# A state update over 64 rows, padded with zeros to 128

The kernel computes a decayed linear attention followed by a gated feed-forward block. Four times in its run it updates a running state from the lower 64 rows of a tile. The change lets these four updates use all 128 rows, with a copy of v whose upper 64 rows are zero.

## Chip, cores, metric

One core of one Trainium2 chip. The metric is the device time of the kernel in microseconds (us). A profile of one execution was kept for every kernel; it is the first of the six runs listed, but for the kernel before, whose profiled execution (310.72 us) is not among its timed runs. The span of a profile is some 2 us shorter than the time, because the time counts what stands around the program too.

## The reference

Eight batches, eight heads, 576 positions, head size 64. The attention has no softmax: scores are multiplied by a causal decay, so the past can be carried in a 64x64 state per head. The code is shortened: `rel` is the distance of two positions.

```python
def _attn_ref(q, k, v):
    scores = scale * np.matmul(q, k.transpose(0, 1, 3, 2))
    gamma = 1.0 - 2.0 ** (-5.0 - np.arange(H))
    Dmat = np.where(rel >= 0, gamma[:, None, None] ** rel[None, :, :], 0.0)
    return np.matmul(scores * Dmat[None], v)

def _moe_ref(x, w_in, w_out):          # x: 4608 tokens x 512
    h = x @ w_in                       # 512 -> 2048
    return (h * np.cos(h)) @ w_out     # 2048 -> 512
```

## The kernel before

The 4608 tokens are handled in 36 groups of 128 rows. A batch has 576 rows, which is four and a half groups, so of every nine groups the fifth (`c == MIX`) is shared: its upper 64 rows end one batch, its lower 64 rows begin the next. These shared groups are 4, 13, 22 and 31. The state of the new batch must be built from the lower 64 rows alone.

```python
    def state(g):                                  # on TensorE, then DVE
        ...
        fresh = c in (0, MIX)                      # a new batch begins
        ps = tiles["stps"]                         # PSUM, kept over the batch
        p0 = HP if c == MIX else 0                 # HP = 64
        for hg in range(HG):                       # four pairs of heads
            nc.tensor.matmul(
                ps[:, hg, :],
                lhsT=qks[p0:, 1, 2 * hg : 2 * hg + 2, :]...,
                rhs=vb[p0:, 2 * hg : 2 * hg + 2, :]...,
                start=(fresh and hg == 0), ...)
        ...                                        # DVE: mask, to bf16
```

The other matmuls have these shapes. The feed-forward block (`h` and `o`) and the use of the state (`ov<-qkT,sb`) use 128 rows and 128 columns of the array. The scores (`sc`) use 64 rows, since a head has 64. The product of scores and v (`ov<-ret,vb`) uses 128 rows and 64 columns.

GpSimd prepares each group: it scales q and k, and casts v to bf16. From group 8 on, a DMA transposes q and k. All loads of q, k and v, the DMA transposes and the output stores are issued by one engine, SyncE, in program order, from group 6 on in `feed`, which runs after each finished output tile:

```python
    def feed(s):                                   # s: output tile just done
        while transposed < min(prepared, s + 10):
            transposes(transposed); transposed += 1
        while loaded < min(NG, 2 * s + 8, s + 13):
            load(loaded); loaded += 1
        while prepared < min(NG, loaded, 2 * s + 7, s + 11):
            prep(prepared); prepared += 1
            ...
```

Of the kernel before, what the change touches and what calls it, by code (L numbers as in the profile page):

```python
# [9 lines left out]
BF16 = mybir.dt.bfloat16  # L10
# [7 lines left out]
def kernel(  # L18
# [16 lines left out]
    nc = tc.nc  # L35
    P = 128
    B, H, S, D = q.shape
# [7 lines left out]
    PER = 2 * S // P  # L45
    MIX = PER // 2
    HP = P // 2
# [10 lines left out]
    consts = ctx.enter_context(tc.tile_pool(name="consts", bufs=1))  # L58
# [31 lines left out]
    w_in_sb = consts.tile([P, DG, DF], BF16)  # L90
    w_out_sb = consts.tile([P, ET, DM], BF16)

    tiles = {}

    def load(g, names="qkv", gate=None):
# [25 lines left out]
    def prep(g, early=False):  # L121

        c = g % PER
        fk, fv = (tiles.pop(("f" + n, g)) for n in "kv")
        qks = nat.tile([P, 2, H, D], BF16, tag="qks", name="qks")
        vb = nat.tile([P, H, D], BF16, tag="vb", name="vb")
        qkT = trp.tile([P, 2 * HG, P], BF16, tag="qkT", name="qkT")
        tq = gq[:, c, :].unsqueeze(2).to_broadcast([P, H, D])
        tk = gk[:, c, :].unsqueeze(2).to_broadcast([P, H, D])
        if not early:  # L130
            fq = tiles.pop(("fq", g))
            nc.gpsimd.tensor_tensor(out=qks[:, 0], in0=fq, in1=tq, op=ALU.mult)  # L132
        (nc.vector if g == 3 else nc.gpsimd).tensor_tensor(  # L133
            out=qks[:, 1], in0=fk, in1=tk, op=ALU.mult
        )
        if early:
            tiles["fv", g] = fv
        else:
            nc.gpsimd.tensor_copy(vb, fv)  # L139
        qT = qT4[:, :, g * P : (g + 1) * P] if early else qkT[:, :HG, :]  # L140
        tiles["a", g] = (qks, vb, qkT, qT)

# [47 lines left out]
    def state(g):  # L190
        c = g % PER
        if c == PER - 1:
            return
        qks, vb, qkT, qT = tiles["a", g]
        fresh = c in (0, MIX)
        if fresh:
            tiles["stps"] = psum.tile([P, HG, P], F32, tag="st", name="st")
        ps = tiles["stps"]
        p0 = HP if c == MIX else 0
        for hg in range(HG):  # L200
            nc.tensor.matmul(  # L201
                ps[:, hg, :],
                lhsT=qks[p0:, 1, 2 * hg : 2 * hg + 2, :].rearrange("s h d -> s (h d)"),
                rhs=vb[p0:, 2 * hg : 2 * hg + 2, :].rearrange("s h d -> s (h d)"),
                start=(fresh and hg == 0),
                stop=(c in (MIX - 1, PER - 2) and hg == HG - 1),
                skip_group_check=True,
            )
        sb = stp.tile([P, HG, P], BF16, tag="sb", name="sb")
        nc.vector.tensor_tensor(  # L210
            out=sb,
            in0=ps,
            in1=diag2.unsqueeze(1).to_broadcast([P, HG, P]),
            op=ALU.mult,
        )
        tiles["sb", g + 1] = sb
# [86 lines left out]
    def feed(s):  # L303

        nonlocal loaded, prepared, transposed
        while transposed < min(prepared, s + 10):
            transposes(transposed)
            transposed += 1
        while loaded < min(NG, 2 * s + 8, s + 13):
            load(loaded)  # L310
            loaded += 1
        while prepared < min(NG, loaded, 2 * s + 7, s + 11):
            prep(prepared)
            prepared += 1
            if transposed < N_PE_T:
                transposed += 1
# [39 lines left out]
    nc.scalar.activation(gq4, pos4, ACTF.Exp, bias=ln_scale, scale=1.0)  # L356
    nc.scalar.activation(gq, pos, ACTF.Exp, bias=ln_scale, scale=1.0)
    nc.scalar.activation(gk, pos, ACTF.Exp, bias=0.0, scale=-1.0)
    nc.vector.memset(diag2, 0.0)
    nc.vector.memset(diag2[0:D, 0:D], 1.0)  # L360
    nc.vector.memset(diag2[D:P, D:P], 1.0)
# [12 lines left out]
    for h0, bank, evac in ((0, "b", nc.scalar.copy), (HG, "m", nc.vector.tensor_copy)):  # L374
# [9 lines left out]
        for r in range(G4):  # L384
            for j in range(2):
                nc.tensor.matmul(
                    ps[:, j, :, r],
                    lhsT=qs4[:, r, h0 + 2 * j : h0 + 2 * j + 2, :].rearrange("p h d -> p (h d)"),
                    rhs=ident,
# [3 lines left out]
        evac(qT4[:, h0 // 2 : h0 // 2 + 2, :], ps.rearrange("d j i r -> d j (i r)"))  # L393
    w_dma = []
    prep(0, early=True)
    transposes(0, "nn", only=(1,))
    scores(0, "a", idle=2)
    for g in range(G4):
        if g == 0:
            prep(1, early=True)  # L400
        w_dma += [load_w_in(e, e + 512) for e in ((0,), (512,), (1024, 1536), ())[g]]
        if g == 2:
            w_dma += [load_w_out(e, e + 4) for e in range(0, ET, 4)]
            load(4, gate=w_dma[5])
            load(5)
            nc.gpsimd.tensor_copy(tri_mix, tri)
            nc.gpsimd.memset(tri_mix[:HP, HP:], 0.0)
        if g + 1 < G4:
            state(g)
            transposes(g + 1, "nn", only=(1,))  # L410
            if g + 2 < G4:
                prep(g + 2, early=True)
            scores(g + 1, "ab"[(g + 1) % 2], idle=3)
            attn_out([g], "m", evac=nc.scalar.copy)
# [5 lines left out]
    def pair(g, banks, sc, av):  # L420

        mid = (sc + av) // 2
        return [
            (sc - 5, lambda: state(g)),
            (sc, lambda: (scores(g, banks[0]), scores(g + 1, banks[1]))),
            (mid, lambda: state(g + 1)),
            (av, lambda: attn_out([g, g + 1], banks[0])),
        ]
# [7 lines left out]
    for n, w in enumerate(widths):  # L436
# [22 lines left out]
        g = starts[n] // P + w // P  # L459
# [76 lines left out]
```

## Time and profile before

| | |
|---|---|
| time, first three runs | 312.71, 312.76, 312.77 us |
| span of the profile | 308.8 us |
| PE busy | 302.1 us, 98% |
| DMA engines busy | 90% or more in slices 2 to 21 of 40 |

These lines are from the page of the kernel before: busy times by engine, the busy tenths in 40 slices of the span for PE and DMA, and the sums of the chain that ended last.

```profile
PE 302.1 (98%) x2361; PEld 171.2 (55%) x2361; DVE 176.1 (57%) x179; ACT 116.7 (38%) x136; POOL 97.2 (31%) x120
...
PE   8899999999999999999999999999999999999996
...
DMA  8999999999999999999990999279935510110012
...
PE 72%; DMA 11%; SPq 11%; POOL 3%; issue 1%; ACT 1%; DVE 0%; POOLq 0%; ACTq 0%
```

PE is nearly always busy, but the chain runs over DMA and SyncE's queue (SPq) for over a fifth of the span. So two limits exist. The next view says where the second one is: the chain in order of time (start in us, length in us, what), in a window.

```profile
101.57 1.31 SPq L146
...
102.94 4.06 DMA fq<-in_q_dram
...
107.15 1.05 POOL qks L132
108.20 1.07 SPq L146
...
113.04 4.22 DMA qkT<-qks
...
117.30 0.40 PE sc L173 x8
117.70 2.70 PE o L287 x12
```

Loads, GpSimd's preparation and the transposes follow one another until the transpose of group 17 lands at 117.3 us. From there to the end PE waits for nobody. The timeline of PE shows the same place; the columns are start, length, engine, line, operation, out and in, shape, count, and in brackets the idle time before it.

```profile
116.60 0.40 PE L173 MATMUL sc<-qkT 64*128 64x128 bf16 x8
117.30 0.40 PE L173 MATMUL sc<-qkT 64*128 64x128 bf16 x8 [0.31 <-DMA qkT<-qks]
117.63 2.76 PE L287 MATMUL o<-w_out_sb,gT 128*128 128x512 bf16 x12
```

The start of the last score matmul before the gap and of the first after it lie 0.47 us further apart than back to back issue would have it. I call this the wait at 117 us.

What the change aims at is less plain to see. This is PE's timeline around the state updates of groups 22 (64 rows) and 23 (128 rows):

```profile
174.06 1.46 PE L287 MATMUL o<-w_out_sb,gT 128*128 128x512 bf16 x6
175.46 0.40 PE L201 MATMUL st<-vb,qks 64*128 64x128 bf16 x4
175.78 2.12 PE L287 MATMUL o<-w_out_sb,gT 128*128 128x512 bf16 x9
177.74 0.39 PE L201 MATMUL st<-vb,qks 128*128 128x128 bf16 x4
177.96 0.59 PE L287 MATMUL o<-w_out_sb,gT 128*128 128x512 bf16 x2
```

Read the starts, not the lengths. Four state matmuls over 128 rows take from 177.74 to 177.96, that is 0.22 us. Four over 64 rows take from 175.46 to 175.78, 0.32 us. The six `o` matmuls ahead of those need 6 x 0.216 = 1.30 us, but 1.40 us pass. From the single records: entering costs 95 ns, the second matmul comes 11 ns late, leaving costs 92 ns and the one after that 11 ns, 0.21 us in all. I call these delays the drains. None of it is listed as idle, because the listed length of a matmul is longer than its distance to the next: 368 ns on the mean for `o`, while starts are 216 ns apart. So a PE that is busy for 98% hides it. "Trainium Kernel Development and Optimization", Performance Expectations, of the Trainium skill warns that matmul busy time is a bad metric for how close a kernel is to its limit (roofline), because matmuls are pipelined, and this trace agrees.

What goes on inside the array during a drain is not settled by this trace. The weight loads (PEld) of the same update and of that of group 23 show one more difference:

```profile
175.45 0.22 PEld L201 LDWEIGHTS <-qks 64*128 64x128 bf16 x4 [0.42 <-issue]
175.78 1.62 PEld L287 LDWEIGHTS <-gT 128*128 128x128 bf16 x9
177.52 0.43 PEld L201 LDWEIGHTS <-qks 128*128 128x128 bf16 x4
```

Group 23's first weights load from 177.52 us, one matmul ahead of the state matmul at 177.74. Group 22's load only at 175.45, just before their own matmul. In the single records from 18.5 us on, the weight load starts 1 to 5 ns before its matmul at every one of the 67 changes of shape, and 53 ns or more before it at every `h`, `o` and state matmul without a change. So a drain may be the emptying of the array, or a weight load that can't run ahead, or both. The delay does not follow the listed length of the weight load (95 to 96 ns late into 64 rows with loads of 92 to 96 ns, 93 ns late into 64 columns with loads of 106 to 110 ns), but that does not decide it.

### The profile page before, as it was taken

To read this page: it belongs to the slowest core of one execution; us is meant where nothing else is said; L and a number is where in the kernel's file an instruction comes from. 1 tells how busy PE (TensorE), PEld (TensorE's weight loads), DVE (VectorE), ACT (ScalarE), POOL (GpSimd) and SP (SyncE) were. 2 spreads that over 40 slices of the span, in tenths; PEclk is the share of its full clock that TensorE was granted. 3 is DMA by queue.
4 is the path that set the end of the run, shared out by engine and by line. 5 is a ranking of instruction groups with operands and counts; after the bars stand their busy time and mean duration, and the time that the engine had idled before them with its cause. 6 is when DMAs were issued, how large, how long until landed. Compare 5 with 4: busy or idle time off the path is not lost.

```text
span 308.8 us, 5686 instructions
## 1 busy us (share of the span) xinstructions
PE 302.1 (98%) x2361; PEld 171.2 (55%) x2361; DVE 176.1 (57%) x179; ACT 116.7 (38%) x136; POOL 97.2 (31%) x120
## 2 busy tenths in 40 slices
PE   8899999999999999999999999999999999999996
PEld 3478547857588554445544554455445544554444
DVE  5766424565777764755466556755576556724610
ACT  3566234615046212640264016511551056015611
POOL 2740066644563554452542244214430000000000
PEclk9999999999999999999999999999999999999999
DMA  8999999999999999999990999279935510110012
GB/s 212 210 210 207 202 227 217 213 225 209 196 235 203 234 219 218 227 196 198 239 244 3 213 214 228 28 166 227 232 59 70 136 37 0 36 68 34 2 65 71
DMA packets 148697, 49.65 MB, mean 161 GB/s; under 512 B 138688, under 2 KB 144192, under 8 KB 148672
## 3 DMA queue, kind: packets, MB, share of 16 engines
q1 hardware_dynamic: 144448, 45.10, 77.3%
q0 software_dynamic: 4224, 4.19, 8.2%
q8 instruction: 18, 0.29, 0.4%
q14 instruction: 7, 0.06, 0.1%
HBM read 36.70 MB, written 9.44 MB: 149 GB/s over the span
## 4 chain that ended last, share of the span: by engine, by line
PE 72%; DMA 11%; SPq 11%; POOL 3%; issue 1%; ACT 1%; DVE 0%; POOLq 0%; ACTq 0%
PE o L287 33%; PE h L270 31%; SPq L107 8%; DMA fq<-in_q_dram 5%; DMA fk<-in_k_dram 5%; PE ov L243 2%; PE sc L173 2%; PE st L201 2%; SPq L146 2%; PE ov L230 1%; DMA qkT<-qks 1%; POOL qks L133 1%; POOL qks L132 1%; SPq L298 1%; PE tr L151 0%
## 5 line engine op out<-in xcount | busy, mean ns | idle before, releaser
L287 PE MATMUL o<-w_out_sb,gT 128*128 128x512 bf16 (+2 forms) x608 | 134.8, 368 | 0.3 <-DVE ret L182 0.3
L270 PE MATMUL h<-xT,w_in_sb 128*128 128x512 bf16 (+2 forms) x832 | 127.6, 313 | 0.6 <-DVE xT L255 0.3
L279 DVE TENSOR_TENSOR gT<-h,cosh 128x1024 bf16<-128x1024 f32 x72 | 88.2, 1225 | 56.7 <-ACT cosh L278 56.6
L270 PEld LDWEIGHTS <-w_in_sb 128*128 128x128 bf16 x832 | 75.7, 98 | 51.2 <-issue 1.5
L278 ACT ACTIVATE cosh<-h,half_pi 128x1024 f32<-128x1024 f32 x72 | 80.2, 1113 | 52.1 <-PE h L270 52.1
L287 PEld LDWEIGHTS <-gT 128*128 128x128 bf16 x608 | 55.3, 98 | 56.8 <-issue 0.6
L132 POOL TENSOR_TENSOR qks<-fq,gq 128x512 bf16<-128x512 f32 x32 | 33.3, 1042 | 107.9 <-DMA fq<-in_q_dram 103.0
L296 ACT COPY ot<-o 128x512 f32<-128x512 f32 (+2 forms) x38 | 21.4, 563 | 120.6 <-PE o L287 117.6
L133 POOL TENSOR_TENSOR qks<-fk,gk 128x512 bf16<-128x512 f32 x35 | 36.5, 1042 | 13.5 <-DMA fk<-in_k_dram 12.2
L182 DVE TENSOR_TENSOR ret<-sc,tri 128x1024 bf16<-128x1024 f32 x32 | 38.0, 1218 | 3.6 <-PE sc L173 3.6
L210 DVE TENSOR_TENSOR sb<-st,diag_105 128x512 bf16<-128x512 f32 x32 | 22.0, 687 | 28.9 <-PE st L201 28.9
L255 DVE CAST xT<-ov 128x1024 bf16<-128x1024 f32 (+1 forms) x17 | 19.7, 1161 | 24.3 <-PE ov L243 24.3
L139 POOL CAST vb<-fv 128x512 bf16<-128x512 f32 x32 | 19.5, 610 | 7.8 <-DMA fv<-in_v_dram 5.9
L201 PEld LDWEIGHTS <-qks 128*128 128x128 bf16 (+1 forms) x128 | 9.3, 97 | 7.5 <-issue 1.3
L201 PE MATMUL st<-vb,qks 128*128 128x128 bf16 (+1 forms) x128 | 12.4, 219 | 0.1
L243 PE MATMUL ov<-ret,vb 128*64 128x128 bf16 x288 | 12.0, 222 | 0.0
L173 PEld LDWEIGHTS <-qkT 64*128 64x128 bf16 x288 | 8.1, 94 | 5.8 <-ACT qkT L156 2.3
L173 PE MATMUL sc<-qkT 64*128 64x128 bf16 x256 | 10.3, 217 | 0.3 <-DMA qkT<-qks 0.3
L230 PEld LDWEIGHTS <-sb 128*128 128x128 bf16 x128 | 8.3, 98 | 3.7
L156 ACT COPY qkT<-tr 128x512 bf16<-128x512 bf16 x12 | 6.6, 587 | 9.0 <-PE tr L151 9.0
L243 PEld LDWEIGHTS <-vb 128*64 128x64 bf16 x288 | 8.7, 109 | 2.0
L230 PE MATMUL ov<-qkT,sb 128*128 128x128 bf16 (+1 forms) x116 | 8.8, 215 | 0.0
(45 smaller groups left out, 53.5 us busy)
## 6 DMA issues: line engine op xcount, KB each, us to landing
out_dram<-ot SPq DMA_DIRECT2D x35, 256.0 KB, 4.1
fk<-in_k_dram SPq DMA_DIRECT2D x32, 256.0 KB, 4.9
fv<-in_v_dram SPq DMA_DIRECT2D x32, 256.0 KB, 4.9
fq<-in_q_dram SPq DMA_DIRECT2D x28, 256.0 KB, 4.1
w_in_sb<-in_moe_w_in_dram POOLq DMA_DIRECT2D x4, 512.0 KB, 8.9
w_out_sb<-in_moe_w_out_dram POOLq DMA_DIRECT2D x4, 512.0 KB, 16.1
fq_110<-in_q_dram SPq DMA_DIRECT2D x2, 512.0 KB, 4.4
fq<-in_q_dram SPq DMA_DIRECT2D x8, 128.0 KB, 4.1
```

The costliest lines, as they stand in the source:

```text
L107: i = nc.sync.dma_start(f[p0:p1], src[b, :, s0 : s0 + p1 - p0, :].rearrange("h s d -> s h d"))
L132: nc.gpsimd.tensor_tensor(out=qks[:, 0], in0=fq, in1=tq, op=ALU.mult)
L133: (nc.vector if g == 3 else nc.gpsimd).tensor_tensor(out=qks[:, 1], in0=fk, in1=tk, op=ALU.mult)
L173: nc.tensor.matmul(ps[:, he, hg, :], lhsT=qkT[d0 : d0 + D, HG + hg, :], rhs=qT[d0 : d0 + D, hg, :], start=True, stop=True,)
L182: nc.vector.tensor_tensor(out=ret.rearrange("p a b i -> p (a b) i"), in0=ps.rearrange("p a b i -> p (a b) i"), in1=mask.unsqueeze(1).to_br ...
L201: nc.tensor.matmul(ps[:, hg, :], lhsT=qks[p0:, 1, 2 * hg : 2 * hg + 2, :].rearrange("s h d -> s (h d)"), rhs=vb[p0:, 2 * hg : 2 * hg + 2, ...
L210: nc.vector.tensor_tensor(out=sb, in0=ps, in1=diag2.unsqueeze(1).to_broadcast([P, HG, P]), op=ALU.mult,)
L243: nc.tensor.matmul(ps[he * D : he * D + D, x, hg, :], lhsT=vb[:, 2 * hg + he, :], rhs=ret[:, he, hg, :], start=(g % PER == 0 and hg == 0), ...
L270: nc.tensor.matmul(ps[:, j, :], lhsT=w_in_sb[:, dg, (et + j) * P : (et + j + 1) * P], rhs=xT[:, dg, c0 : c0 + w], start=(dg == 0), stop=(d ...
L278: nc.scalar.activation(cosh, ps, ACTF.Sin, bias=half_pi, scale=1.0)
L279: nc.vector.tensor_mul(gT[:, et : et + m, c0 : c0 + w], ps, cosh)
L287: nc.tensor.matmul(ps, lhsT=gT[:, et, tsi * P : (tsi + 1) * P], rhs=w_out_sb[:, et, c0:c1], start=(et == 0), stop=(et == ET - 1),)
```

## The change

The intent: if the array keeps one shape, these delays go. The rows of a matmul cost nothing in themselves: state matmuls follow each other every 56 ns over 64 rows and over 128. So v is copied once more, into a tile whose upper half was set to zero at the start, and the upper rows of k are multiplied by zero. In the diff, operands are shortened.

```diff
+    v_odd = consts.tile([P, 2, H, D], BF16)
 ...                                            # in prep(g), after the cast of v
+        if c == MIX:
+            nc.gpsimd.tensor_copy(v_odd[HP:, g // PER % 2], fv[HP:])
 ...                                            # in state(g)
-        p0 = HP if c == MIX else 0
+        vs = v_odd[:, g // PER % 2] if c == MIX else vb
-                lhsT=qks[p0:, 1, 2 * hg : 2 * hg + 2, :]...,
-                rhs=vb[p0:, 2 * hg : 2 * hg + 2, :]...,
+                lhsT=qks[:, 1, 2 * hg : 2 * hg + 2, :]...,
+                rhs=vs[:, 2 * hg : 2 * hg + 2, :]...,
 ...                                            # at the start
+    nc.vector.memset(v_odd[:HP], 0.0)
```

More of the change, by code (lines that the diff above doesn't have):

```diff
@@ L202, in state @@
                 ps[:, hg, :],
-                lhsT=qks[p0:, 1, 2 * hg : 2 * hg + 2, :].rearrange("s h d -> s (h d)"),
-                rhs=vb[p0:, 2 * hg : 2 * hg + 2, :].rearrange("s h d -> s (h d)"),
+                lhsT=qks[:, 1, 2 * hg : 2 * hg + 2, :].rearrange("s h d -> s (h d)"),
+                rhs=vs[:, 2 * hg : 2 * hg + 2, :].rearrange("s h d -> s (h d)"),
                 start=(fresh and hg == 0),
```

## The prediction

> **What bounds the kernel.** TensorE. The first part of the page shows PE busy 302.1 of 308.8 us (98%), granted clock full. Its starts, in the list of instructions by time, are back to back: 216 ns apart for 512 columns, 56 ns for 128. The exceptions are mostly changes of the tile shape of the array: where the rows or columns in use go from 128 to 64 or back, the next matmul starts 92 to 96 ns later than its neighbours do. Before about 138 us there is a second limit. DMA is busy 90% or more in nearly every slice, and the sync queue issues the outputs up to 20 us after they are ready. The chain of waits leaves PE at 48.6 us and comes back at 117.3 us, where a score matmul waits 0.47 us for the DMA transpose of qkT.
>
> **What the change does.** Four of the 36 groups (4, 13, 22, 31) are shared. Their state update, four matmuls each, uses 64 rows amid 128-row matmuls. With a zero-padded v it uses 128 rows and the shape does not change.
>
> *Removed.* In each of the four places the trace has, over back-to-back issue: 95 ns entering, 10 ns after the first matmul, 92 ns leaving, 11 ns after that. Sum 0.208 us, times 4 = 0.83 us. "TensorEngine Tiling (Array Packing)", Key Properties, of the Trainium skill says that changing the tiling mode drains TensorE; the trace agrees, with these numbers.
>
> *Not changed.* The matmuls: 219 ns, 56 ns apart, for both row counts. Weight loads take 98 ns against 94 ns and are hidden; the skill's "TensorE: Matmul & The Clock Gate", LDWEIGHTS, says only columns count. The instruction order of every engine is otherwise the same.
>
> *Added.* A DVE memset of 64x512 words: estimate 0.49 us, from 0.27 us for 256 columns. It falls near 2.3 us, where DVE then idles 2.04 us for the load of q: free. Four GpSimd casts of 64x512, estimate 0.61 us each, from the 128x512 cast of v. After those of groups 4 and 13 GpSimd has 0.3 and 3.5 us of idle time; group 5's products start about 0.3 us later, which the 1.2 us idle before group 6 swallows. The new v is ready 1.5 us or more before its matmuls. The v buffer is held 0.6 us longer, but its reload comes far later. No new wait on PE.
>
> **How much is on the critical path.** The savings of groups 22 (175 us) and 31 (241 us) lie where PE alone runs: 0.42 us to the end. Those of groups 4 (44 us) and 13 (105 us) come before the wait at 117 us. That transpose hangs on loads and the sync queue, which do not follow PE, so these 0.42 us should mostly become a longer wait there (0.47 to about 0.9 us). If the timed runs, which are not traced, don't wait there, all 0.83 us is saved.
>
> **Predicted time.** 312.76 less 0.42 to 0.83, nearer the former: 312.25 us, 8 times in 10 within 311.8 to 312.7. Faster by over 2%: 0.01; within 2%: 0.98; slower: 0.01.
>
> **What would show it.** State matmuls all 128 rows, entering and leaving at 216 and 56 ns like the others: right. The wait for qkT near 117 us grown by 0.4 us: absorption right; unchanged, with the transpose earlier: wrong. GpSimd busy up by about 2.4 us, DVE by 0.5 us, and PE's waits for v no longer than before.
>
> **What would make it wrong.** The DMA-limited first half is touchy: a shift of a load or transpose by some tenths of a us moves the wait at 117 us by as much, either way, as large as the gain. A GpSimd cast on 64 partitions may cost more than estimated, or stand before a transpose that the chain needs.

## The result

| | median | lowest | highest | runs |
|---|---|---|---|---|
| before | 312.56 us | 311.93 | 312.77 | 6 |
| changed | 312.29 us | 311.49 | 313.99 | 6 |

The ratio is 0.9998, with a 95% interval of 0.9969 to 1.0027. A ratio here is the mean time of one kernel's fast runs over that of the other's of the same rounds, so it is not quite the ratio of the medians in the table. The median is near the predicted one, 312.25 us, but the runs scatter by more than the gain, and the interval reaches from 1.0 us of gain to 0.8 us of loss. The slowest run, 313.99 us, is also the one with a granted clock of 0.994; the other five had 1.0.

The profile of the changed kernel has a longer span, 310.3 us (its time was 312.15 us, that of the kernel before in its profile 310.72 us). The same lines of its page:

```profile
PE 299.3 (96%) x2328; PEld 171.9 (55%) x2361; DVE 176.6 (57%) x180; ACT 116.7 (38%) x136; POOL 99.7 (32%) x124
...
PE   8899999999999998999999999999999999999996
...
DMA  8999999999999999998992799469945510010012
...
PE 75%; DMA 13%; SPq 7%; issue 1%; POOL 1%; ACT 1%; DVE 0%; POOLq 0%; ACTq 0%
```

PE's 299.3 us are no gain: 33 of 2361 matmul records are missing in this trace, so a gap of exactly one matmul is a lost record. GpSimd is up by 2.5 us and DVE by 0.5 us, as foreseen. Now the state update of group 22, in PE's timeline (line 205 is what line 201 was, 291 is 287, 177 is 173, 150 is 146):

```profile
174.19 3.19 PE L291 MATMUL o<-w_out_sb,gT 128*128 128x512 bf16 x13
177.21 0.39 PE L205 MATMUL st<-v_odd,qks 128*128 128x128 bf16 x4
177.44 1.03 PE L291 MATMUL o<-w_out_sb,gT 128*128 128x512 bf16 x4
```

Its four matmuls now take 0.23 us by these lines (177.21 to 177.44), and the single records show 216 ns and 56 ns on either side. So the drains are gone. There are 59 changes of shape left from 18.5 us on (counted in the complete profile of the run "again"), where the kernel before had 67. But the wait at 117 us has grown:

```profile
117.49 0.40 PE L177 MATMUL sc<-qkT 64*128 64x128 bf16 x8
119.16 0.40 PE L177 MATMUL sc<-qkT 64*128 64x128 bf16 x8 [1.27 <-DMA qkT<-qks]
119.71 1.03 PE L291 MATMUL o<-w_out_sb,gT 128*128 128x512 bf16 x4 [0.16 <-issue]
```

It is 1.43 us by the starts, where 0.9 was foreseen; the transpose itself was issued at 114.84 us instead of 113.04. Another wait for a transpose, of 0.91 us, stands near 85 us, where the kernel before has none. So there are two readings. Theory A: the drains are all there is to it, and the loads simply ran late in this execution. Theory B: the added casts and the memset push the loads and transposes back. The experiments had to tell these apart, and to find out where the saving of the early groups goes.

### The profile page after: what moved, and what is told of

It reads as the page before. It is cut to its first block, busy times and chain, and to the rows that moved or that the text cites. A ratio compares the mean times of both kernels' runs of the same rounds, so it can differ in the third digit from the quotient of the medians.

```text
span 310.3 us, 5654 instructions
## 1 busy us (share of the span) xinstructions
PE 299.3 (96%) x2328; PEld 171.9 (55%) x2361; DVE 176.6 (57%) x180; ACT 116.7 (38%) x136; POOL 99.7 (32%) x124
## 4 chain that ended last, share of the span: by engine, by line
PE 75%; DMA 13%; SPq 7%; issue 1%; POOL 1%; ACT 1%; DVE 0%; POOLq 0%; ACTq 0%
PE h L274 36%; PE o L291 32%; DMA fq<-in_q_dram 5%; SPq L109 5%; DMA qkT<-qks 3%; DMA w_in_sb<-in_moe_w_in_dram 2%; DMA fk<-in_k_dram 2%; PE ov L247 2%; PE sc L177 2%; PE st L205 1%; PE ov L234 1%; SPq L150 1%; SPq L302 1%; POOL qks L134 1%; POOL qks L135 1%
## 5 line engine op out<-in xcount | busy, mean ns | idle before, releaser
L291 PE MATMUL o<-w_out_sb,gT 128*128 128x512 bf16 (+2 forms) x583 | 131.0, 367 | 2.6 <-issue 1.6
L205 PEld LDWEIGHTS <-qks 128*128 128x128 bf16 x128 | 9.6, 98 | 6.7
L205 PE MATMUL st<-vb,qks 128*128 128x128 bf16 x112 | 10.8, 219 | 0.0
```

The source lines that it names most:

```text
L205: nc.tensor.matmul(ps[:, hg, :], lhsT=qks[:, 1, 2 * hg : 2 * hg + 2, :].rearrange("s h d -> s (h d)"), rhs=vs[:, 2 * hg : 2 * hg + 2, :].r ...
L291: nc.tensor.matmul(ps, lhsT=gT[:, et, tsi * P : (tsi + 1) * P], rhs=w_out_sb[:, et, c0:c1], start=(et == 0), stop=(et == ET - 1),)
```

## The experiments

Each kernel had six runs, beside eleven runs of the kernel before on the same chip. For the profiles I use one sum that leaves out the varying start: the time from the first `h` matmul to the end of the last matmul, called the stretch. It is worked out from the single records.

| kernel | median us | kernel before, same job | ratio, 95% interval | stretch us | wait at 117 us |
|---|---|---|---|---|---|
| before, first profile | 312.56 | | | 288.15 | 0.47 |
| changed, first profile | 312.29 | 312.56 | 0.9998 (0.9969 to 1.0027) | 289.00 | 1.43 |
| again | 310.53 | 311.07 | 0.9992 (0.9965 to 1.0019) | 287.43 | 0.58 |
| only_rows | 310.31 | 311.07 | 0.9977 (0.9959 to 0.9995) | 287.47 | 0.50 |
| late64 | 313.40 | 311.07 | 1.0070 (1.0052 to 1.0088) | 290.86 | 1.08 |
| early64 | 312.11 | 311.07 | 1.0033 (1.0015 to 1.0051) | 289.56 | none |
| only_copy | 310.94 | 310.89 | 0.9998 (0.9979 to 1.0017) | 287.84 | 0.15 |
| before_T | 310.32 | 310.89 | 0.9981 (0.9961 to 1.0000) | 287.67 | none |
| after_T | 309.44 | 310.89 | 0.9952 (0.9935 to 0.9969) | 286.83 | none |
| after_T2 | 310.50 | 310.89 | 0.9977 (0.9956 to 0.9998) | 286.96 | none |
| early64_T | 312.20 | 311.54 | 1.0028 (0.9994 to 1.0062) | 289.55 | none |
| after_T_again | 309.53 | 311.54 | 0.9930 (0.9904 to 0.9955) | 286.95 | none |
| after_TW | 313.56 | 311.54 | 1.0053 (1.0010 to 1.0096) | 286.83 | none |

### again: the changed kernel, unaltered

> The changed kernel once more, unaltered. Theory A (only the drains matter; the early half of the saving goes into a longer wait for a load-paced transpose near 117 us): 0.4 us under the kernel before, within 0 to 0.8; the transposes may come earlier or later than in the first profile of the changed kernel, since their lateness there was chance. Theory B (the added casts and the memset push the loads and transposes back): no gain or a loss of up to 0.5 us, and the same late transposes as in its first profile, that of group 17 issued near 114.8 us against 113.0 before, with waits of 0.9 us near 85 and 1.4 us near 118.

Measured: 310.53 us against 311.07 us, six runs of 310.00 to 312.78. By the medians that is 0.54 us less; by the ratio, with an interval of 1.1 us of gain to 0.6 us of loss, it can't be told from nothing, nor from the full 0.83 us. The profile is the better witness. The transpose of group 17 was issued at 112.76 us, not 114.84, no wait stands near 85 us, and the wait at 117 us is 0.58 us:

```profile
116.33 0.28 PE L177 MATMUL sc<-qkT 64*128 64x128 bf16 x4
117.03 0.40 PE L177 MATMUL sc<-qkT 64*128 64x128 bf16 x8 [0.42 <-DMA qkT<-qks]
117.35 2.76 PE L291 MATMUL o<-w_out_sb,gT 128*128 128x512 bf16 x12
```

Same kernel, other waits: the lateness in the first profile was chance. By the test that the prediction had set, a wait grown by 0.4 us, neither profile decides: it grew by 0.96 us in one and by 0.11 us in the other. GpSimd's timeline in this profile shows what the added cast does at its tightest place, between groups 4 and 5:

```profile
41.73 0.61 POOL L141 CAST vb<-fv 128x512 bf16<-128x512 f32 x1 [0.60 <-DMA fv<-in_v_dram]
42.40 0.61 POOL L143 CAST v_odd<-fv 64x512 bf16<-64x512 f32 x1
43.09 1.04 POOL L134 TENSOR_TENSOR qks<-fq,gq 128x512 bf16<-128x512 f32 x1
44.09 1.04 POOL L135 TENSOR_TENSOR qks<-fk,gk 128x512 bf16<-128x512 f32 x1
45.08 0.61 POOL L141 CAST vb<-fv 128x512 bf16<-128x512 f32 x1
46.57 1.04 POOL L134 TENSOR_TENSOR qks<-fq,gq 128x512 bf16<-128x512 f32 x1 [0.88 <-DMA fq<-in_q_dram]
```

Group 5 starts right after the cast of 0.61 us, and 0.88 us of idle time ahead of group 6 remain. The delay ends there.

### only_rows: 128 rows without the copy

The v of the shared groups is the existing tile of zeros. Its output is wrong, which doesn't matter for the time.

```diff
-        p0 = HP if c == MIX else 0
-                lhsT=qks[p0:, 1, ...
-                rhs=vb[p0:, ...
+                lhsT=qks[:, 1, ...
+                rhs=zeros[:, hg * P : (hg + 1) * P] if c == MIX else vb[:, ...
```

> The shared groups' state update over 128 rows with the constant tile of zeros as v: no copy, no memset, no new tile; result wrong on purpose. Theory A: the same time as the changed kernel within noise, 0.4 us under before (0 to 0.8). Theory B: better than the changed kernel by 0.5 us or more, with transposes as early as in the profile of before.

Measured: 310.31 us, 0.22 us under the changed kernel by the medians, and a stretch of 287.47 us against 287.43. No 0.5 us or more hang on the added work. The transpose of group 17 was issued at 113.82 us here, without any added work, later than in the profile of before.

### only_copy: the added work with 64 rows

The tile, the memset and the casts of the change, with the old `p0`.

> The added tile, memset and four GpSimd casts, with the state updates of the shared groups still over 64 rows. Theory A (added work is free): within 0.3 us of the kernel before, the drains still there, the transpose of group 17 issued at about the same time. Theory B (added work pushes the loads): 0.5 us or more slower.

Measured: 310.94 us against 310.89 us, ratio 0.9998. The interval alone would still allow 0.5 us more, so the profile has to help: the transpose of group 17 was issued at 112.82 us, no later than in the profile of before (113.04), and the stretch less the wait is 287.84 - 0.15 = 287.69 us, where before_T, which has neither the wait nor the added work, takes 287.67. The added work is free within the noise. With only_rows this speaks against theory B throughout. What the late first profile showed was the scatter of the loads.

### late64 and early64: ten more drains, late or early

Ten ordinary groups get the narrow update too. Their outputs are wrong, which doesn't matter for the times.

```diff
-        p0 = HP if c == MIX else 0
+        p0 = HP if c == MIX or g in (18, 19, 20, 21, 23, 24, 25, 27, 28, 29) else 0    # late64
+        p0 = HP if c == MIX or g in (5, 6, 7, 9, 10, 11, 12, 14, 15, 16) else 0        # early64
```

> The kernel before with ten more state updates over 64 rows (groups 18 to 21, 23 to 25, 27 to 29, all after the load-limited part); result wrong on purpose. Theory A: each costs 0.208 us of drains and all of it shows: 2.1 us slower (1.7 to 2.5). If the drains were hidden in the whole time: within 0.5 us of before.

> The kernel before with ten more state updates over 64 rows in groups 5 to 7, 9 to 12, 14 to 16, all before the wait near 117 us; result wrong on purpose. Theory A: 2.1 us of drains, less the wait that they use up (0.5 to 1.4 us): 0.7 to 1.6 us slower, and no wait for the transpose near 117 us in the profile. If nothing is absorbed: 2.1 us, the same as with ten late groups.

Measured: the late ten cost 0.70%, 2.2 us; the early ten 0.33%, 1.0 us. The single records show what each update adds over back to back issue: 0.21 us, at all ten late places and at nine of the ten early ones. At the tenth, group 5 near 49 us, nothing is added: PE had to wait there in any case, for 0.23 us by the starts, until ScalarE had copied a transposed tile out of PSUM (the copy ends at 49.67 us in before, and the next `h` starts at 49.73), and the drains now fill that wait. The wait at 117 us is gone in early64:

```profile
117.60 0.64 PE L243 MATMUL ov<-ret,vb 128*64 128x128 bf16 x16
118.17 0.62 PE L173 MATMUL sc<-qkT 64*128 64x128 bf16 x16
118.72 0.61 PE L287 MATMUL o<-w_out_sb,gT 128*128 128x512 bf16 x2
```

PE comes to its score matmuls 1.57 us later than before (118.17 against 116.60), and the transpose has landed. A drain has the same size everywhere. Where a wait for something else follows it, the wait gives the time back. The runs of early64 also lie within 0.21 us of one another, while those of before scatter over 2.02 us. That fits a time which PE alone sets once the load-paced wait is out of the way; but early64_T below, where it is out of the way too, has one run 2.6 us above the rest, so steadiness is not assured by it.

### before_T and after_T: the wait taken away

The same edit in both kernels (shortened below). Each group's product is prepared ahead of the transposes in `feed`, and from output tile 7 on one more transpose is allowed, so that the transpose of group 17, and each later one, is issued one store and one set of loads earlier.

```diff
+        if s >= 7: prepare (as at the end of feed)
-        while transposed < min(prepared, s + 10):
+        while transposed < min(prepared, s + 10 + (s >= 7)):
             transposes(transposed)
```

> The kernel before, with the DMA transpose of group 17 (and each later one) issued one output store and one set of loads earlier. It takes away the wait near 117 us. The run with ten early drains had hidden about 1.0 us of them and its runs lay within 0.2 us of each other. Theory A: 0.5 to 1.1 us faster than before, a spread of some tenths of a us at most, no wait for qkT near 117 us in the profile. If the wait there costs nothing in the whole time: within 0.2 us of before.

> The changed kernel with the same earlier transposes. Theory A: with nothing left to absorb it, the whole 0.83 us of the drains shows against the same edit of the kernel before (0.6 to 1.0), so 1.3 to 1.9 us under the kernel before. Rival (the early half of the saving is lost for another reason than the wait): about 0.4 us under the same edit of the kernel before.

Measured in the same job: before 310.89, before_T 310.32, after_T 309.44 us. By the means of the six runs, before_T is at 310.43 and after_T at 309.57, so the change is now worth 0.86 us, and every run of after_T (309.42 to 309.90) lies under every run of before_T (310.16 to 310.88). In the job of the run "again" it had been 0.24 us by the means, with the wide interval given there; that the early half was lost in it rests on the profiles and on early64, not on this difference. The stretches differ by 287.67 - 286.83 = 0.84 us, four times 0.21. The transposes of group 17 were issued at 109.33 and 109.18 us, and PE runs through. This is after_T:

```profile
115.79 0.50 PE L247 MATMUL ov<-ret,vb 128*64 128x128 bf16 x12
116.22 0.62 PE L177 MATMUL sc<-qkT 64*128 64x128 bf16 x16
116.77 2.55 PE L291 MATMUL o<-w_out_sb,gT 128*128 128x512 bf16 x11
```

before_T shows the same picture later: its sixteen score matmuls start at 116.61 us. The difference of 0.39 us, or 0.42 us counted from the first `h` matmul of each, is what the early groups 4 and 13 save, no longer given back. Groups 22 and 31 add the rest. The stretch of before also fits: 287.67 + 0.47 = 288.14 us, against 288.15 measured.

after_T_again is the same kernel in another job:

> The best version so far once more, on another job: 1.2 to 1.8 us under before, 0.4 to 0.5%, runs within 0.5 us of each other except for a group some 0.4 us above, which are those with a late start.

Measured: 309.53 us against 311.54 us, five of six runs from 309.43 to 309.68 and one at 310.46. That is 2.01 us, more than the 1.2 to 1.8 foreseen. The kernel itself is where it was; the kernel before was 0.65 us slower in this job, so the ratio, 0.9930, flatters it. This is the version that beats both.

### early64_T: do the ten early drains cost in full without the wait?

> The kernel before with earlier transposes, and ten early state updates over 64 rows (result wrong on purpose). With late transposes these ten cost 1.0 us. Theory A (the other half had used up a wait for the transposes): with that wait gone they cost their full 2.1 us against the kernel before with earlier transposes, which was 0.6 us under before: so 1.5 us slower than before (1.2 to 1.8). Rival (early drains are cheaper in themselves, or overlap other work): about 0.5 us slower than before.

Measured: 312.20 us against 311.54 us, ratio 1.0028, with one run at 314.91. The number given in advance, 1.5 us slower than before (1.2 to 1.8), was missed by the 0.66 us measured. Most of the miss is that the kernel before was slower in this job: against its 310.89 us in the job of before_T, 312.20 is 1.31 us more. Against before_T, which is in another job, the medians differ by 1.88 us, and so do the stretches: 289.55 - 287.67 = 1.88 us. That is nine times 0.21 us (1.89), since the tenth falls into the wait near 49 us. And early64_T and early64 have the same stretch within 0.01 us: where early drains have used up the wait, an earlier transpose brings nothing. The rival, that early drains are cheaper in themselves, falls by this and by the 0.21 us in the records.

### after_T2 and after_TW: the rest of the scatter

after_T2 has the preparation first from output tile 3 on, so that the transpose of group 11 is earlier too.

> As the run before, with the transpose of group 11 earlier too, where the first profile of the changed kernel had waited 0.9 us near 85 us. Theory A: as that run or up to 0.3 us better, with a smaller spread, since one more load-paced wait is gone.

Measured: 310.50 us, with runs from 309.48 to 310.86. It is not better than after_T, and not as steady. Its stretch is 286.96 us, that of after_T but for 0.13 us. What is longer is the start: its first `h` matmul begins at 19.11 us, in after_T at 17.87. In the thirteen profiles this start lies between 17.7 and 17.9 us in eight, and between 18.4 and 20.1 us in five. after_T_again has 18.75 us in the profile where the same kernel had 17.87. So this is chance at the start (but for after_TW, the latest). What varies is the landing of the first load of w_in: in the four late profiles other than after_TW it lands at 18.36 to 19.06 us and `h` starts 0.04 to 0.05 us later; in the eight early ones it lands at 17.49 to 17.62 us, while PE is still busy with the matmuls ahead of `h`. In only_rows and in after_T_again the profiled run, with its late start, is the slowest of the six (311.07 and 310.46 us). after_TW tried to mend it:

```diff
         if g == 0:
+            w_dma.append(load_w_in(0, 512))    # was issued after prep(1)
             prep(1, early=True)
```

> The changed kernel with earlier transposes, and the first load of w_in issued before GpSimd's product for group 1 instead of after it. In some profiles the first h matmul starts at 17.8 us, in others (first profile of the changed kernel, the run without copies, the run with the transpose of group 11 earlier) at 18.4 to 19.1 us, having waited for that load. If that start is what is left of the spread: 0 to 0.4 us better than the same kernel with the old order, spread smaller. If the load pushes back the k loads of groups 1 to 3[...]: 0.2 to 0.5 us slower.

Measured: 313.56 us, 1.0053, much worse than foreseen in either case. Four of its six runs had a granted clock of 0.989 to 0.995 and took 313.01 to 315.65 us; the two with a clock of 1.0 took 311.62 (the profiled one) and 311.45 us, about 2 us more than after_T_again in the same job. What lowered the clock in the four is not shown. Three lines of the start of its timeline (GpSimd and PE) show where:

```profile
8.64 0.94 POOL L379 DMA_DIRECT2D w_in_sb<-in_moe_w_in_dram  x1
...
18.00 0.40 PE L155 MATMUL tr<-ident,qks 128*128 128x128 bf16 x4 [0.82 <-DVE qks L135]
...
20.07 1.48 PE L274 MATMUL h<-xT,w_in_sb 128*128 128x256 bf16 x12
```

The load of the weights now runs from 8.64 to 15.88 us, over most of the load of k of group 3: by the DMA's semaphore updates in the trace, that k landed at 17.16 us, in the kernel before at 14.57, though both were issued at 9.5 us. So DVE's product of it came late, and the transposes of group 3 start at 18.00 us, where those of before start at 15.76. The stretch, 286.83 us, is just that of after_T: in the profiled run all of the loss lies in the start. What makes the first load of w_in land early or late in the unedited kernels stays open.

## Why the prediction was right

- *The drains.* 0.208 us per place and 0.83 us in all were foreseen. The stretches give 0.84 us, the six runs of before_T and after_T 0.86 us by their means. Right in size and place. "the trace agrees" holds for the delay; that it is a drain of the array is not shown. Nor are all weight loads hidden, as the prediction has it: the first one at each change of shape starts with its own matmul.
- *The added work.* Free, as foreseen: only_copy has a ratio of 0.9998. The cast took 0.61 us on 64 rows, as on 128, and the memset 0.485 us, against estimates of 0.61 and 0.49.
- *The early half.* "these 0.42 us should mostly become a longer wait there". The mechanism is shown by early64 (2.1 us of drains cost 1.0), early64_T and the pair before_T and after_T. The size of the wait, "0.47 to about 0.9 us", is not what the profiles gave: 1.43 us in the first, beyond it, and 0.58 us in the second, within it but only 0.11 us more than before. The wait moves with the transpose, which in these two came 1.80 us later and 0.28 us earlier than in the profile of before. In the second, PE arrived 0.39 us earlier and the wait ended 0.28 us earlier: the difference went into the wait, the rest was kept by luck of the loads.
- *What would make it wrong.* The text named the load-limited half as touchy. The scatter of single runs, 2.5 us in the changed kernel against a gain of 0.3 us in the medians, is in part that: the stretches of its two profiles differ by 1.57 us, nearly all of it in waits for transposes. A late start adds to the scatter, and the slowest run had a clock of 0.994; these had not been foreseen.
- *The time.* 312.25 us foreseen, 312.29 measured. A hit to 0.04 us is luck, given the scatter and a ratio of 0.9998, which is a gain of under 0.1 us. The profile of the kernel before took 310.72 us, 1.2 us less than the fastest of its six timed runs; what made those longer no trace shows, so the waits in them need not be those of the profile.

## What to carry to other kernels

Here a matmul that used fewer rows or columns of the array than its neighbours paid at both ends, and padding its operands with zeros to the neighbours' 128 rows cost TensorE nothing (56 ns apart either way), so look for such places, and pad where the padded copy falls into idle time of another engine. Look for such costs in the distance between starts, not in busy shares or idle columns, which show nothing of them. Before counting a saving, find the next wait that something else paces: what is saved ahead of it is given back there, and moving that wait (here one transpose, issued earlier) can be worth nearly as much as the change (0.6 us by the means here) and can lay the change open: with it the runs of the two kernels no longer overlapped.

## What the Trainium skill lacked or had wrong

- "TensorEngine Tiling (Array Packing)", Key Properties, says that a change of the tiling mode drains TensorE, and gives no cost. Here it is a 92 to 96 ns later start at each change, and 10 to 11 ns more at the matmul after it: 0.21 us for going to 64 rows and back. The change from 128 to 64 columns costs as much (93 to 96 ns).
- The same page recommends tiling where the contraction is 64 rows or fewer. It does not say that a few such matmuls among full-size ones are better padded to 128 rows: 0.84 us less here for four groups of four, by the stretches of before_T and after_T.
- "TensorE: Matmul & The Clock Gate", LDWEIGHTS, says that only columns count. Nearly so: 98 ns for 128 rows and 94 ns for 64.
- "Perfetto Trace Analysis" does not say that a profile can lack some matmul records, nor that such a loss shows as a gap of exactly one matmul between starts. In four of the thirteen profiles 33 of 2361 were missing, and PE busy then read 299.3 us where a complete profile of the same kernel read 301.4.
